# Weight conversions in other steps, operands split ahead by way of DRAM, sums spaced out: one change to a fused attention and two-MLP kernel

## The chip, the cores and the metric

The kernel runs on one core of a Trainium2 chip. The metric is device microseconds of one execution, the median of several. TensorE multiplies matrices (PE in the rows; PEld is its weight load, which runs beside it), VectorE (DVE), ScalarE (ACT) and GpSimd (POOL) work element by element, and DMA transfers are issued from the queues of SyncE (SPq) and ScalarE (ACTq).

## The reference

```python
# q, k, v: (8, 8, 576, 64);  w_in: (512, 2048);  w_out: (2048, 512), twice; the weights arrive as 64-bit floats
q_s = exp(q - max(q, -1));  q_s = q_s / (sum(q_s, -1) + 1e-9)
k_s = exp(k - max(k, 2));   k_s = k_s / (sum(k_s, 2) + 1e-9)
kv  = einsum('bhsd,bhse->bhde', k_s, v)
x   = einsum('bhsd,bhde->bhse', q_s, kv)       # then (4608 tokens, 512)
h = x @ w_in;   x = (h * clip(h + 3, 0, 6) / 6) @ w_out        # first MLP
h = x @ w2_in;  out = (h * sigmoid(h)) @ w2_out                # second MLP
```

## The kernel before

**Precision.** A float32 operand is split into an upper part, rounded to TensorE's reduced format by a copy on ScalarE, and a lower part, the rest, by a subtraction on VectorE. Each product is three matmuls (upper by upper, upper by lower, lower by upper), each 128x128 by 128x512.

**First MLP** (up to about 957 us). Tokens go in 9 blocks of 512. A block takes 16 steps, one for each 128 columns of `w_in`. A step holds `mm1` (L485, 12 matmuls of L492), `gate` (L542: Relu on ScalarE L505, product on VectorE L512, upper part on ScalarE L520, lower part on VectorE L523), and `mm2` of the step before (L551, 12 matmuls of L562). Steps are numbered 0 to 15 within a block here. Everything is emitted in program order, and each engine works in that order.

Attention runs inside these steps, one unit (a pair of heads for one block) for every four steps. A unit begins in step 1, 5, 9 or 13, and its part number r counts steps from there. At r = 0, after the gate, `k_max` (L285) makes VectorE find the maxima of k, which the transposition `k_turn` (L294, L296) on TensorE takes at r = 1, right after that step's `mm1`. At r = 3 (steps 0, 4, 8 and 12), `q_store` (L416) sends a transposed tile to DRAM from ScalarE's queue (zd<-qz, L417). At r = 4 (steps 1, 5, 9 and 13) ScalarE, at the top of its step, waits for that store, issues `q_load`'s four loads (qt<-zd, L423), scales a small tile (`kv_upper`, L353), and only then comes to the Relu of the step. From the third block on, r = 4 of a unit and r = 0 of the next one fall in the same step.

In the same steps the weights of the second MLP are prepared, two jobs a block (`Parts`, L172). A job converts two tiles from 64 bits (`convert`: two ScalarE passes L114 and L116, three VectorE passes L120, L127 and L131), makes four sums on GpSimd (`sums`, L196), and splits and stores four tiles (`upper` L202, `lower` L206 and L208, ws<-sp). `load_w` fetches the raw tiles (L97, wi_raw).

**Second MLP** (957 to 1721 us). Tokens go in four pairs of blocks, and each pair does its two matrix products by a scheme with 7 block products in place of 8 (`second_mlp`, L960). A pair has an inner stage (L991, w2_in) and an outer stage (L1089, w2_out) of 56 product steps each, six matmuls to a step. Work is put at planned times in units of such a step, with `when(t, fn)`, and emitted in the order of these times; t0 is the start of a pair, start[0] that of its outer stage. In the outer stage every step needs its own moving operand split first: `split` (ScalarE, L1070) and `split_low` (VectorE, L978, gsp<-g) stand `LOOK` = 3 steps ahead. GpSimd turns the stored tiles into the next products' operands (T2 and T4) inside `split_low`, and `join` combines finished products on VectorE, all of one product at once. The outer stage also prepares the 14 operand tiles of the next pair, `op[name]` (`x_steps`, L905): it loads them from `yd` (L893), sums on GpSimd (L903, 128x1024), and splits in place (L899 ScalarE, L900 VectorE, xo). Weights stream through six ring tiles of 512 KB, refilled when used (`fetch`, L875, ring<-ws). `spare` holds eight 128x512 tiles. A last block goes through the second MLP in the plain way, from about 1626 us.

## Time and profile before

| | us |
|---|---|
| median of 3 runs (1722.03 to 1725.01) | 1724.02 |
| the profiled execution | 1723.13 |
| its span in the profile | 1721.3 |
| PE busy | 1631.2 (95%) |
| DVE busy | 1080.8 (63%) |
| ACT busy | 741.7 (43%) |
| POOL busy | 357.4 (21%) |

The 1.8 us between span and execution lie around the program. TensorE is busy in all but 90 us, so a wait elsewhere matters where TensorE ends up waiting for it. Its granted clock is 0.986 of full speed over the span.

### The profile page before, as it was taken

Reading aid. Unit: us, or ns where it says so; the run is one execution under the profiler, and the core shown is the slowest. Engines: PE = TensorE matmul, PEld = TensorE weight load, DVE = VectorE, ACT = ScalarE, POOL = GpSimd, SP = SyncE. Lnnn points to the kernel's source line nnn. Section 1 sums busy time; section 2 is a strip of 40 time slices with the busy share of each in tenths; the row PEclk is TensorE's granted clock in tenths of the full one; section 3 lists DMA queues with packets and bytes.
Section 4 is the critical chain, followed back from the end, with each engine's and each line's share of the span. In section 5 each row is a group of like instructions: output and inputs, shape, how many; then the busy total and the mean of one; then the engine's idle time right before and its main releaser. Section 6 shows DMA issues by size and latency. Waiting matters only on the chain.

```text
span 1721.3 us, 21607 instructions
## 1 busy us (share of the span) xinstructions
PE 1631.2 (95%) x7612; PEld 1312.2 (76%) x7612; DVE 1080.8 (63%) x1748; ACT 741.7 (43%) x1285; POOL 357.4 (21%) x290
## 2 busy tenths in 40 slices
PE   6999999898998989989999999899999999999998
PEld 4777777677876777878788886788678867886887
DVE  8997556565564556555545568856885687568522
ACT  6885334343443434333334434434443444344322
POOL 2111101111011110111111127112701370135000
PEclk9999999999999999999999999999999999999999
DMA  9812434444443445323342656466546655669730
GB/s 274 299 41 65 138 107 125 113 132 126 139 121 96 134 110 162 118 76 103 98 159 74 220 191 213 163 205 215 212 163 208 204 208 176 210 204 348 259 122 25
DMA packets 273498, 273.53 MB, mean 159 GB/s; under 512 B 111216, under 2 KB 195184, under 8 KB 273392
## 3 DMA queue, kind: packets, MB, share of 16 engines
q1 hardware_dynamic: 210432, 256.92, 45.3%
q10 hardware_dynamic: 62960, 15.25, 3.9%
q8 instruction: 60, 0.98, 0.2%
q14 instruction: 46, 0.38, 0.1%
HBM read 212.60 MB, written 59.51 MB: 158 GB/s over the span
## 4 chain that ended last, share of the span: by engine, by line
PE 70%; DVE 17%; ACT 4%; DMA 4%; issue 2%; POOL 1%; ACTq 1%; SPq 0%; DVEq 0%; POOLq 0%
PE h L492 19%; PE y L562 17%; PE pb L991 17%; PE pb L1089 11%; DVE gsp L978 5%; PE y L564 2%; DMA zd<-qz 2%; DVE fa L127 2%; PE pa L450 1%; DVE fa L131 1%; DMA qt<-zd 1%; DVE r L512 1%; DVE xo L900 1%; ACTq L423 1%; DVE g L523 1%
## 5 line engine op out<-in xcount | busy, mean ns | idle before, releaser
L492 PE MATMUL h<-x,wi 128*128 128x512 f32 x1920 | 472.6, 393 | 2.3 <-DVE wi L152 1.0
L562 PE MATMUL y<-g,wo 128*128 128x512 f32 x1728 | 432.6, 400 | 2.4 <-ACT g L520 2.4
L492 PEld LDWEIGHTS h<-x,wi 128*128 128x128 f32 x1920 | 356.6, 188 | 79.3 <-DVE wi L152 2.8
L562 PEld LDWEIGHTS y<-g,wo 128*128 128x128 f32 x1728 | 329.6, 193 | 73.4 <-ACT g L520 2.8
L1089 PE MATMUL pb<-gsp,ring 128*128 128x512 f32 x1344 | 326.2, 399 | 24.8 <-DVE gsp L978 20.9
L1089 PEld LDWEIGHTS pb<-gsp,ring 128*128 128x128 f32 x1344 | 251.8, 190 | 97.9 <-DVE gsp L978 43.3
L991 PE MATMUL pb<-xo,ring 128*128 128x512 f32 x1344 | 313.3, 391 | 0.0
L991 PEld LDWEIGHTS pb<-xo,ring 128*128 128x128 f32 x1344 | 250.5, 188 | 51.7
L512 DVE SCALAR_TENSOR_TENSOR r<-r,h 128x512 f32<-128x512 f32 x128 | 87.9, 687 | 231.4 <-ACT r L505 230.8
L978 DVE TENSOR_TENSOR gsp<-g,gsp 128x512 fp32r<-128x512 f32 x192 | 178.8, 957 | 40.9 <-ACT gsp L1070 40.5
L1070 ACT CAST gsp<-g 128x512 fp32r<-128x512 f32 x192 | 117.0, 620 | 108.2 <-PE pb L1089 74.3
L505 ACT ACTIVATE r<-h 128x512 f32<-128x512 f32 x144 | 85.9, 597 | 169.7 <-PE h L492 164.6
L520 ACT CAST g<-r 128x512 fp32r<-128x512 f32 x144 | 89.4, 621 | 143.1 <-DVE r L512 131.0
L523 DVE TENSOR_TENSOR g<-r,g 128x512 fp32r<-128x512 f32 x144 | 103.1, 716 | 53.4 <-ACT g L520 43.8
L978 POOL TENSOR_TENSOR spare<-g,g 128x512 f32<-128x512 f32 x32 | 43.2, 1351 | 352.0 <-DVE g L978 315.2
L978 DVE TENSOR_TENSOR g<-r,pb 128x512 f32<-128x512 f32 x96 | 65.9, 686 | 70.8 <-ACT r L1004 70.4
L375 POOL TENSOR_TENSOR qe<-qraw,qm 128x512 f32<-128x512 f32 x34 | 36.0, 1058 | 352.4 <-DVE qm L367 281.7
L397 POOL TENSOR_TENSOR qe<-qe,qs 128x512 f32<-128x512 f32 x36 | 37.6, 1045 | 315.3 <-DVE qs L392 311.2
L1004 ACT ACTIVATE r<-pb 128x512 f32<-128x512 f32 x96 | 57.5, 599 | 91.1 <-DVE pb L978 74.8
L120 DVE TENSOR_SCALAR fa<-fa 128x512 uint32<-128x512 uint32 x64 | 28.0, 438 | 69.5 <-ACT fa L114 69.2
L353 ACT ACTIVATE kv<-pa,rs 64x64 fp32r<-64x64 f32 x56 | 17.3, 309 | 105.1 <-DMA qt<-zd 49.0
L978 DVE TENSOR_TENSOR U<-pb,s 128x512 f32<-128x512 f32 x64 | 44.2, 691 | 24.1 <-PE pb L991 22.3
(150 smaller groups left out, 1608.4 us busy)
## 6 DMA issues: line engine op xcount, KB each, us to landing
ring<-ws SPq DMA_DIRECT2D x224, 512.0 KB, 3.7
ws<-sp SPq DMA_DIRECT2D x128, 256.0 KB, 2.5
yd<-o SPq DMA_DIRECT2D x36, 256.0 KB, 2.9
wi_early<-in_moe_w_in_dram SPq DMA_DIRECT2D x16, 512.0 KB, 9.0
wo_early<-in_moe_w_out_dram SPq DMA_DIRECT2D x16, 512.0 KB, 9.4
wi_raw<-in_moe_w_in_dram SPq DMA_DIRECT2D x16, 512.0 KB, 4.4
wo_raw<-in_moe_w_out_dram SPq DMA_DIRECT2D x16, 512.0 KB, 4.1
out_dram<-o SPq DMA_DIRECT2D x32, 256.0 KB, 3.2
```

Of the source, the lines that this page charges most:

```text
L397: eng.tensor_tensor(out=e, in0=e, in1=s.to_broadcast([P, 2 * NCH, D]), op=ALU.mult)
L492: nc.tensor.matmul(h, w[:, a, c, :], x[:, e, c, :], start=(c == 0 and n == 0), stop=(c == NC - 1 and n == 2),)
L505: nc.scalar.activation(self.r, self.h, AF.Relu, bias=3.0)
L512: nc.vector.scalar_tensor_tensor(out=r, in0=r, scalar=6.0, in1=h, op0=ALU.min, op1=ALU.mult)
L520: nc.scalar.copy(self.g[:, 0], self.r)
L523: nc.vector.tensor_tensor(out=self.g[:, 1], in0=self.r, in1=f32(self.g[:, 0]), op=ALU.subtract)
L562: nc.tensor.matmul(y[c], w[:, a, cs], g[:, e, :], start=st, stop=sp)
L978: (eng or nc.vector).tensor_tensor(out=out, in0=a, in1=b, op=how)
L991: nc.tensor.matmul(to, ws_[:, a], e[:, c], start=p in ("P1", "P6", "P5") and c == 0 and m == 0, stop=c == 1 and m == 2, skip_group_check=True,
L1004: nc.scalar.activation(r, d[b, n, key], AF.Sigmoid)
L1070: nc.scalar.copy(t[:, 0], source(p, i))
L1089: nc.tensor.matmul(d[b, p][m], w[:, a, m * P : (m + 1) * P], t[:, e], start=i == 0 and k == 0, stop=i == NPR - 1 and k == 2, skip_group_ch ...
```

## The change

Three things are done, and the order of TensorE's instructions stays the same.

1. In the first MLP a job's conversions stand in steps 3 and 4, and 11 and 12, of each block's 16, where they stood in 1 and 2, and 8 and 9. The four sums follow in the second conversion's step, and the four splits and stores take that step and the three after it (before: 4 to 7 and 11 to 14). `load_w` moves along.
2. In the second MLP the next pair's operands are made in halves (`x_ahead`): four loads into `spare`, four GpSimd sums (128x512), seven splits into the rotating tiles of the outer splits, and 14 stores to a new DRAM buffer `xd`. For the second pair both halves are made in the first pair's inner stage. For later pairs the first half is made in the outer stage of two pairs before, the second in the inner stage of the pair before. 14 transfers (`x_fetch`) then bring the finished operands into `op` in the outer stage.
3. The T2 and T4 sums go to planned times of their own (`next_t2` every 1.8 steps, `next_t4` every 2.6), `c22` moves from VectorE to GpSimd, the joins are one step apart, splits stand 4 steps ahead over five tiles in place of four.

```diff
+    xd = dram.tile([2, 7, P, 2, 2, BLK], F32, name="xd")
...
-    LOOK = 3
+    LOOK = 4
...
-                add(d[b, n, "22"], d.pop((b, n, "U3")), d[b, n, "22"])
+                add(d[b, n, "22"], d.pop((b, n, "U3")), d[b, n, "22"], ALU.add, nc.gpsimd)
...
-            when(e["P7"] + 1.1, lambda: sig(b, n, "22"))
+            when(e["P7"] + 1.6, lambda: sig(b, n, "22"))
...
+        def split_tile():
+            n = turns[0] % 5
+            turns[0] += 1
+            if n == 4:
+                return [
+                    att.tile([P, BLK], F32R, tag=tag, bufs=1, name="gsp") for tag in ("ke", "qe")
+                ]
+            if n < 2:
                 t = gs.tile([P, 2, BLK], F32R, tag="g", name="gsp")
             else:
+                t = att.tile([P, 2, BLK], F32R, tag=("sp", "qT")[n - 2], bufs=1, name="gsp")
+            return [t[:, 0], t[:, 1]]
...
         def split_low(b, p, i):
             t = d["sp", b, p, i]
-            add(t[:, 1], source(p, i), f32(t[:, 0]), ALU.subtract)
-            if p == "P1":
-                g1 = g_of(2 * i)
-                add(g1[:, 0], op["spare"][:, i], g1[:, 0], ALU.add, nc.gpsimd)
-            if p == "P6":
...
+            add(t[1], source(p, i), f32(t[0]), ALU.subtract)
+
+        def next_t2(i):
+            g1 = g_of(2 * i)
+            add(g1[:, 0], op["spare"][:, i], g1[:, 0], ALU.add, nc.gpsimd)
...
+        def x_ahead(j, c, side, t, step):
+
+            st = {n: op["spare"][:, 3 + m] for m, n in enumerate(("B12", "B22", "B11", "B21", "T"))}
+
+            def load(n):
+                jj, h = j + (n[2] == "2"), int(n[1] == "2")
+                nc.sync.dma_start(st[n], yd[jj, 2 * h + c])
+
+            def high(n, src):
+                d["x", n] = split_tile()
+                nc.scalar.copy(d["x", n][0], st[src])
+
+            def low(n, src):
+                hi, lo = d.pop(("x", n))
+                add(lo, st[src], f32(hi), ALU.subtract)
+                to = xd[side, XS.index(n)]
+                nc.sync.dma_start(to[:, 0, c], f32(hi))
+                nc.sync.dma_start(to[:, 1, c], f32(lo))
...
+                when(t + m * step + 0.3, lambda n=n, src=src: high(n, src))
+                when(t + m * step + 0.9, lambda n=n, src=src: low(n, src))
+
+        def x_fetch(side, n, low):
+            nc.sync.dma_start(f32(op[n][low]), xd[side, XS.index(n)][:, low])
...
+                if p == "P1":
+                    when(start[0] + 1.4 + 1.8 * i, lambda i=i: next_t2(i))
+                if p == "P6":
+                    when(start[0] + 18.4 + 2.6 * i, lambda i=i: next_t4(i))
...
+                if b == 0:
+                    x_ahead(j + 2, 0, side, t0 + 1.0, 1.8)
+                    x_ahead(j + 2, 1, side, t0 + 15.0, 1.8)
+                else:
+                    x_ahead(j + 2, 1, side, t0 + 4.0, 3.2)
+                if b + 2 < BB:
+                    x_ahead(j + 4, 0, 1 - side, start[0] + 22.0, 4.0)
+                for m, n in enumerate(XS):
+                    for low in range(2):
+                        when(
+                            start[0] + 3.1 + 6.0 * m + 3.0 * low,
+                            lambda n=n, low=low, side=side: x_fetch(side, n, low),
+                        )
...
-            for r in range(7):
-                parts_at[(n // 2 + 1) * NF + 1 + 7 * (n % 2) + r] = (n, r)
+            for r in range(5):
+                parts_at[(n // 2 + 1) * NF + 3 + 8 * (n % 2) + r] = (n, r)
...
-            if r is not None and r >= 3:
-                made[job].upper(r - 3)
-                made[job].lower(r - 3)
+            if r:
+                made[job].upper(r - 1)
+                made[job].lower(r - 1)
```

Line numbers of the changed kernel are one higher up to about line 1060. On ScalarE, in steps 8 and 9 of a block before the change, k's exponential (L326) is followed by a conversion, the gate, the store, the loads and a second conversion ahead of the next Relu (L505):

```order
L326 ACTIVATE ke<-ke 128x640
L114 ACTIVATE fa<-wi_raw 128x512
L116 ACTIVATE fr<-wi_raw 128x512
L505 ACTIVATE r<-h 128x512
L520 CAST g<-r 128x512
L417 DMA zd<-qz 128x512
L423 DMA qt<-zd 32x16x32 x4
L353 ACTIVATE kv_93<-pa,rs 64x64 x2
L114 ACTIVATE fa<-wi_raw 128x512
L116 ACTIVATE fr<-wi_raw 128x512
L505 ACTIVATE r<-h 128x512
```

The same two steps after the change have neither conversion:

```order
L327 ACTIVATE ke<-ke 128x640
L506 ACTIVATE r<-h 128x512
L521 CAST g<-r 128x512
L418 DMA zd<-qz 128x512
L424 DMA qt<-zd 32x16x32 x4
L354 ACTIVATE kv_93<-pa,rs 64x64 x2
L506 ACTIVATE r<-h 128x512
```

After the change the conversions stand in the two steps that end with another unit's store (here steps 3 and 4, likewise 11 and 12), and the first split (L203) follows the store:

```order
L461 CAST x<-pa 128x512
L115 ACTIVATE fa<-wi_raw 128x512
L117 ACTIVATE fr<-wi_raw 128x512
L506 ACTIVATE r<-h 128x512
L521 CAST g<-r 128x512
L327 ACTIVATE ke<-ke 128x640
L115 ACTIVATE fa<-wi_raw 128x512
L117 ACTIVATE fr<-wi_raw 128x512
L506 ACTIVATE r<-h 128x512
L521 CAST g<-r 128x512
L418 DMA zd<-qz 128x512
L203 CAST sp<-fa 128x512
```

So no conversion stands any more behind a store's wait; one stands ahead of the store in steps 4 and 12. On VectorE, in the outer stage of the first pair before the change, the 1024-wide splits of the next pair's operands (L900) stand between the outer splits (gsp):

```order
L978 TENSOR_TENSOR gsp<-g_8615,gsp 128x512
L900 TENSOR_TENSOR xo<-spare,xo 128x1024
L978 TENSOR_TENSOR gsp<-g_8691,gsp 128x512
L978 TENSOR_TENSOR gsp<-g_8770,gsp 128x512
L978 TENSOR_TENSOR gsp<-g_8238,gsp 128x512
L978 TENSOR_TENSOR gsp<-g_8313,gsp 128x512
L900 TENSOR_TENSOR xo<-spare,xo 128x1024
```

After the change 18 outer splits follow each other here, and from then on half-size splits for a later pair (gsp<-spare, 128x512) and joins (vbuf, fin, kbuf) come in between:

```order
L979 TENSOR_TENSOR gsp<-g_8356,gsp 128x512
L979 TENSOR_TENSOR gsp<-spare,gsp 128x512
L979 TENSOR_TENSOR gsp<-g_8450,gsp 128x512
L979 TENSOR_TENSOR gsp<-g_8548,gsp 128x512
L979 TENSOR_TENSOR vbuf_95<-pb,kbuf_94 128x512
L979 TENSOR_TENSOR gsp<-g_8629,gsp 128x512
L979 TENSOR_TENSOR fin<-pb,fin 128x512
```

The 1024-wide operations have left this stage; the half-size ones stand in its second part, in the first two pairs.

## Rows read from the trace of the kernel before

**Rows 1.** Waits of PE, whole run: us in total, times, longest.
```profile
PE pa L296 <- DVE m L291: 37.1, 11, 5.9
PE pb L1089 <- DVE gsp L978: 20.9, 16, 2.3
PE y L562 <- ACT g L520: 2.4, 1, 2.4
```

**Rows 2.** PE's timeline: start, us, instruction, count, idle before it.
```profile
172.09 2.88 PE L492 MATMUL h<-x,wi 128*128 128x512 f32 x12
186.80 0.27 PE L296 MATMUL pa<-ident,m 128*128 128x128 f32 x1
196.13 2.88 PE L492 MATMUL h<-x,wi 128*128 128x512 f32 x12
216.50 0.44 PE L296 MATMUL pa<-ident,m 128*128 128x128 f32 x1 [5.50 <-DVE m L291]
```

**Rows 3.** Windows behind the first and the last long wait: busy times, PEclk, DMA.
```profile
216.50:222.00 5.50, 5.50 (x20) 4.57 (x21) 3.03 (x7) 1.17 (x3) 1.05 (x1) 0.70 0.02 4
741.00:747.00 6.00, 6.00 (x20) 4.88 (x20) 2.88 (x7) 1.24 (x3) 1.04 (x1) 0.63 0.00 0
```

**Rows 4.** The chain that ended last, 201 to 217 us: start, us, what.
```profile
201.49 4.60 DMA zd<-qz
...
206.74 2.11 DMA qt<-zd
...
209.54 0.66 ACT fa L114
210.20 0.58 ACT fr L116
...
211.53 0.69 DVE fa L131
...
216.06 0.30 DVE m L291
```

**Rows 5.** ACT's timeline, a step's store and loads without a conversion.
```profile
176.42 0.34 ACTq L417 DMA_DIRECT2D zd<-qz  x1
...
178.47 2.92 ACTq L423 DMA_DIRECT2D qt<-zd  x4
```

**Rows 6.** DVE's timeline, the end of `k_max` in that step.
```profile
186.15 0.29 DVE L291 TENSOR_TENSOR m<-m,kbuf 128x128 f32<-128x128 f32 x1
```

**Rows 7.** SP's timeline ahead of the store at 201.49.
```profile
200.91 0.37 SPq L97 DMA_DIRECT2D wi_raw<-in_moe_w_in_dram  x1
```

**Rows 8.** Windows of the first, second and fourth pair: PE, PEld, DVE, ACT, POOL busy, PEclk, DMA.
```profile
962.44:1125.18 162.74, 153.86 (x662) 122.81 (x661) 120.51 (x150) 70.83 (x115) 58.14 (x36) 1.00 0.57 197
1125.18:1294.59 169.41, 162.91 (x706) 129.87 (x705) 120.72 (x150) 73.24 (x121) 58.17 (x36) 0.98 0.58 199
...
1463.98:1625.91 161.93, 159.21 (x706) 128.41 (x705) 109.07 (x147) 69.29 (x118) 46.28 (x32) 1.00 0.76 259
```

**Rows 9.** The chain that ended last, inner stages.
```profile
962.44 70.73 PE pb L991 x312
...
1137.92 0.44 PE pb L1125 x4
```

**Rows 10.** DVE's timeline, outer stage of the first pair.
```profile
1069.42 7.94 DVE L978 TENSOR_TENSOR gsp<-g,gsp 128x512 fp32r<-128x512 f32 x4
```

**Rows 11.** Windows there, and in the fourth pair's outer stage; columns as in rows 8.
```profile
1068.00:1077.00 9.00, 5.10 (x19) 3.33 (x19) 8.72 (x5) 4.51 (x8) 9.00 (x6) 1.00 0.25 72
...
1560.00:1590.00 30.00, 27.56 (x118) 21.58 (x118) 24.51 (x30) 14.08 (x24) 12.10 (x8) 1.00 0.99 353
```

**Rows 12.** Tile gsp, VectorE: ns of one, min/median/max.
```profile
L978 DVE TENSOR_TENSOR gsp<-g,gsp x192: 675/692/2895, 1031.6 to 1621.2; 128x512 fp32r<-128x512 f32 x192
```

**Rows 13.** A GpSimd sum in the page's costliest groups: busy us, mean ns of one, idle before.
```profile
L978 POOL TENSOR_TENSOR spare<-g,g 128x512 f32<-128x512 f32 x32 | 43.2, 1351 | 352.0 <-DVE g L978 315.2
```

**Rows 14.** DMA issues of the page: KB each, median us from issue to landing.
```profile
ring<-ws SPq DMA_DIRECT2D x224, 512.0 KB, 3.7
```

More of the change, by code (lines that the diff above doesn't have):

```diff
@@ new lines, in next_t2, with next_t4, total @@
+        def next_t2(i):
+            g1 = g_of(2 * i)
+            add(g1[:, 0], op["spare"][:, i], g1[:, 0], ALU.add, nc.gpsimd)
+        def next_t4(i):
+            g1 = g_of(2 * i)
+            add(g1[:, 0], g1[:, 0], g_of(2 * i + 1)[:, 0], ALU.subtract, nc.gpsimd)
+        XS = ("B11", "T2", "T1", "B21", "T3", "B22", "T4")
+        def x_ahead(j, c, side, t, step):
[12 more added lines that the diff above has]
+                nc.sync.dma_start(to[:, 1, c], f32(lo))
+            def total(to, x, y, how):
+                add(st[to], st[x], st[y], how, nc.gpsimd)
+            for m, n in enumerate(("B22", "B12", "B11", "B21")):
+                when(t - 4.0 + 0.3 * m, lambda n=n: load(n))
+            when(t + 0.02, lambda: total("T", "B22", "B12", ALU.subtract))
+            when(t + 0.03, lambda: total("B12", "B12", "B11", ALU.subtract))
+            when(t + 3 * step + 0.02, lambda: total("T", "T", "B11", ALU.add))
+            when(t + 5 * step + 0.02, lambda: total("T", "B21", "T", ALU.subtract))
+            for m, (n, src) in enumerate((
+                ("B22", "B22"), ("B11", "B11"), ("T3", "T"), ("T1", "B12"), ("T2", "T"),
+                ("B21", "B21"), ("T4", "T"),
+            )):
+                when(t + m * step + 0.3, lambda n=n, src=src: high(n, src))
+                when(t + m * step + 0.9, lambda n=n, src=src: low(n, src))
@@ L1093, in outer, with joins, tile, do @@
                     )
-        def join(b, p):
-            for m in range(2):
+        def joins(b, p, t):
+            def tile(m, n):
+                return fixed[4 * m + n]
+            def do(m, name):
                 one, two, three, c22 = fixed[4 * m : 4 * m + 4]
-                if p == "P1":
-                    nc.scalar.copy(one, d[b, p][m])
-                if p == "P6":
-                    add(two, d[b, p][m], one)
-                    add(three, d[b, "P7"][m], two)
-                if p == "P5":
-                    add(c22, d[b, p][m], three)
-                    add(two, d[b, p][m], two)
-                if p == "P3":
-                    add(two, d[b, p][m], two)
-                if p == "P4":
-                    add(three, three, d[b, p][m], ALU.subtract)
-                if p == "P2":
-                    add(one, d[b, p][m], one)
-            if p != "P7":
-                d.pop((b, p))
-            if p == "P6":
-                d.pop((b, "P7"))
+                at = d[b, p][m]
+                if name == "one":
+                    nc.scalar.copy(one, at)
+                elif name == "U2":
+                    add(two, at, one)
+                elif name == "U3":
+                    add(three, d[b, "P7"][m], two)
+                elif name == "C22":
+                    add(c22, at, three)
+                elif name in ("U4", "C12"):
+                    add(two, at, two)
+                elif name == "C21":
+                    add(three, three, at, ALU.subtract)
+                else:
+                    add(one, at, one)
+            names = {
+                "P1": ("one",), "P7": (), "P6": ("U2", "U3"), "P5": ("C22", "U4"),
+                "P3": ("C12",), "P4": ("C21",), "P2": ("C11",),
+            }[p]
+            for k, (name, m) in enumerate((name, m) for name in names for m in range(2)):
+                when(t + k, lambda m=m, name=name: do(m, name))
         def turn(j, k, bank=bank):
@@ L1166, in second_mlp @@
                 if i == NPR - 1:
-                    when(t + 1.3, lambda b=b, p=p: join(b, p))
+                    joins(b, p, t + 1.3)
             j = 1 + 2 * b
             if b + 1 < BB:
-                do = x_steps(j + 2)
-                base = start[0]
-                for x, name in (
[3 rows of a table removed]
-                ):
-                    when(base + x, do[name])
+                side = b % 2
+                if b == 0:
+                    x_ahead(j + 2, 0, side, t0 + 1.0, 1.8)
+                    x_ahead(j + 2, 1, side, t0 + 15.0, 1.8)
+                else:
+                    x_ahead(j + 2, 1, side, t0 + 4.0, 3.2)
[7 more added lines that the diff above has]
+                        )
                 for k in range(2 * NCH):
```

24 lines of the change are left out of this document (10 added, 14 removed), and 3 rows, old and new, of the table base.

## The prediction

> **What bounds the kernel now.** I read the page's table of engines first: TensorE is busy in all but 90 us, and the change leaves its instructions and their order alone. So the time can only change where TensorE waits or runs slowly, and the next views were the waits of TensorE and the windows with its clock.
>
> In the first MLP one wait carries nearly everything: `k_turn` waits for the end of `k_max`, 11 times, 37.1 us, and one `mm2` adds 2.4 [rows 1]. Six of the 11 last about 5.5 us, once a block, five about 0.8. Behind each long one the granted clock falls to its lower level for some microseconds: 0.70 over 5.5 us behind the first, 0.63 over 6 us behind the last [rows 3]. While TensorE is busy all the time, a window of length L at mean clock c loses (1 - c)L: 1.7 and 2.2 us for these two, 13.4 for all six. **The first MLP thus holds 37.1 + 2.4 + 13.4 = 52.9 us.**
>
> The chain shows what is late [rows 4]. The store at 201.49 takes 4.60 us to land, the four loads are issued until 208.85, then ScalarE converts (0.66 + 0.58) ahead of the Relu, VectorE works through the conversion ahead of the gate's product, and `k_max`, last in that queue, ends at 216.36. TensorE was there at 211.00 [rows 2]. Step 5 shows the same without a conversion: store at 176.42, 4.33 us after its step's first matmul; landing seen 2.05 us later; loads issued until 181.39 [rows 5]; `k_max` done at 186.44 [rows 6]; TensorE there at 186.80 [rows 2]. That is 0.36 us to spare, 14.71 us after the start of the store's step.
>
> In the second MLP I compare a pair with its matmuls. 312 of them took 70.73 us, 0.2267 each, and a transposition group 0.44 [rows 9]. 672 matmuls and eight groups make 155.9. The second pair takes 169.4, so 13.5 too much; the third is like it; the fourth has 6.0; the first has 660 matmuls and no groups in its window, 149.6, so 13.1 [rows 8]. **Together 46.1 us.** 20.9 of it are waits for `split_low` [rows 1], the clock's 0.98 takes 3.4 in each of two pairs [rows 8], the rest is spread over shorter delays. The cause is in the outer stage: four splits took 7.94 us, 1.99 each [rows 10], where the median is 0.692 [rows 12], in a stretch in which GpSimd was busy without a gap [rows 11]. There VectorE cannot give TensorE one split in each product step of six matmuls, 1.36 us.
>
> **The conversions.** Removed from steps 1, 2, 8 and 9: both late sequences above lose their conversion behind the store. What remains in steps 1 and 9 is step 5's sequence, and without the split that step 5 has ahead of `k_max` (about 0.7). It waits only when the store lands over 1 us later than 2.05. I take nothing for these steps. Their old length, 52.9, is the gain.
>
> What is added stands in steps 4 and 12. There a conversion now comes ahead of the gate whose end starts the store, as it does today in step 8, where the store came 201.49 - 196.13 = 5.36 us after the first matmul [rows 2, 4], so 1.03 later than 4.33. Of these, 0.36 are spare: **0.67 us of new wait**, in each place with a `k_turn` behind it. Units 9, 11, ... 29 make 11 such places: 7.4 us. The low bound is nothing (the split ahead of k's subtraction is gone from the step before, which lets the conversion start earlier). The high bound is a store that lands as today's late one, 4.60 in place of 2.05: 3.2 us in each place, 35 in all. I stay near the low end, for the reason under the first rival. Waits this short would leave the clock where it is, as the short waits of today do. The sums move to the end of steps 4 and 12, where they slow the gate's VectorE operations, not `k_max`; that is inside the bounds. **Net: 52.9 - 7.4 = 45.5 us gained.**
>
> **The operands.** Gone from each outer stage of three pairs are seven 1024-wide splits on VectorE and ScalarE and four 1024-wide sums on GpSimd. In the stretch of rows 10 this was what kept GpSimd busy without a gap. Their work returns as twice as many operations of half the width, most of it in the inner stages, where TensorE waits for nothing; there VectorE was busy 120.5 us of the first pair's 162.7 over both stages [rows 8], and `c22` leaves it. In the outer stages of the first two pairs seven half-size splits remain, from step 22.
>
> I count that stretch, steps 22 to 37, 20.4 us long: 15 outer splits, 4 half-size ones and 8 joins on VectorE, 27 operations of 0.69, 18.6 us; beside them 6 T4 sums and 3 others, 12.2 us at 1.351 [rows 13]. With GpSimd busy throughout, a split costs 1.3 more than its median [rows 10, 12]. Let the stretch take T: T = 18.6 + 19 x 1.3 x 12.2/T gives 29 us, 8.6 too long. Splits run 3.8 steps ahead, 5.2 us, less about 1.6 for the two operations of one: 3.6 to spare. So up to 5 us of wait in each of these pairs, down to none if the overlap costs half as much; I take 3. In the last two pairs (no half-size splits) the same formula gives 22.8 us, within the lead. At the start of every outer stage the T2 sums (8 x 1.351 in 19 us) still slow the splits, though the lead is a step longer; I leave 3 us a pair.
>
> The Trainium skill's page "SBUF — State Buffer", section "SBUF: two separate sides", says that VectorE with two SBUF inputs and a reading GpSimd exclude each other for whole instructions. That agrees with 1.99, which is 0.69 plus about one sum. By the rule the stretch would take 25 us (splits and sums in turn) to 31 (joins too), a wait of 1 to 7 us where I take 3.
>
> **The transfers.** Per pair 8 loads and 28 stores of 256 KB and 14 fetches of 512 KB are added, and 4 loads of 512 KB go. The ring alone moves 512 KB in two steps, 193 GB/s. In the first pair's inner stage, steps 0 to 27, loads and stores add 9.4 MB in 36.7 us: 450 GB/s. The trace sustains 353 [rows 11]. The surplus is 3.6 MB, a delay of 10 us at the end. A ring tile is refilled five tiles, 13.6 us, before use and lands in 3.7 [rows 14], so 9.9 are spare. I take 2 us, bounds 0 and 6. In the outer stages of the first two pairs the sum is 417 GB/s over 34 us, a delay of 6 us, hidden. SyncE's queue is in order: a store waits for its split, and ring refills wait behind it; that uses the same 9.9 us.
>
> Left over: 4 x 3 + 2 x 3 + 2 = 20 us. **Net: 46.1 - 20 = 26.1 us gained.** The joins, spread out, are in the count above.
>
> **Sum.** 1723.13 - 45.5 - 26.1 = 1651.5 for an execution like the profiled one. The median lies 0.9 higher: 1652.
>
> **Rivals.**
>
> *The store lands late in the new place* (steps 4 and 12). Today's late store followed a raw-weight load by 0.6 us [rows 4, 7]. After the change such a load is still issued near this store. For it: it is the same pair of transfers. Against it: on SyncE's queue the load follows that of k, which waits for a subtraction of the step before, so it should start some 2 us or more ahead of the store. Price: 11 x 3.2 = 35 in place of 7.4, so 1680. The Trainium skill's page "DMA: Bandwidth & Descriptors", section "Queues, rings and completion order", says that a DMA engine's signal of completion lands after all its earlier writes, of other queues too; the 4.60 agrees.
>
> *The outer stages keep their excess*: GpSimd and VectorE still collide (T2, T4 and half-size splits), the clock falls again. With 40 of 46.1 left: 1672. With both rivals at once 1700.
>
> *Slower: the transfers become the bound of the first three pairs.* They would move 143 MB there (ring 88, fetches 22, stores 22, the rest 10), in some 501 us today. To lose the 45.5 of the first MLP and 3.4 more, these pairs must take 550 us, so the engines must deliver under 260 GB/s. Against it: 353 over 30 us [rows 11]. For it: a queue in order, in which one late store holds all refills. From 260 down it decides; at 250 the time is about 1745.
>
> **How the numbers follow.** 64% for the forecast, whose own range is 1638 to 1666; 14% for the late store, 14% for the kept excess, 4% for both, 4% for slower. A difference of 0.2%, 3.4 us, is about what a measurement here can tell. Only the last case, and a share of the one before that goes worse than counted, end at or above 1720: faster 0.93, same 0.02, slower 0.05. The range reaches down to no new waits and half the left-over (1637, say 1636) and up past the two middle rivals: 1690.
>
> **What would show it.** Right: the six 5.5 us waits and the lower clock behind them are gone, 11 small waits of `k_turn` at most, no GpSimd operation of 1024, pair windows of about 158, 162, 159 and 159 us. Wrong: waits of `k_turn` of 2 us and more, TensorE waiting for the ring or for `split_low` from step 22 on, the clock below 1 in an outer stage.

## The result, and the profile after

The changed kernel takes 1661.47 us (median of 4 runs), the kernel before 1723.13 beside it: a ratio of 0.964, 95% interval 0.9623 to 0.9656. The forecast was 1652 us. The profiled execution's span fell from 1721.3 to 1660.3 us.

The waits of TensorE in the changed kernel, which answer to [rows 1]:

```profile
engine line waited for: us in total, times, longest us
PE ph L297 <- DVE m L292: 8.5, 3, 7.4
PE pa L297 <- DVE m L292: 7.4, 18, 1.0
PE pb L992 <- DVE U L979: 6.8, 1, 6.8
PE pb L1142 <- DVE gsp L979: 3.4, 6, 1.0
...
PE pb L1142 <- ACT gsp L1081: 1.7, 3, 0.7
```

The six waits of 5.5 us for `k_max` are gone (pa, 7.4 us in all, none over 1.0), and so is most of the waiting for `split_low` (3.4 for 20.9). New is one wait of 6.8 us for U, in the first inner stage. The windows of the first MLP and of the four pairs, with the columns of [rows 8]:

```profile
170.00:906.00 736.00, 728.59 (x3615) 592.99 (x3614) 443.31 (x810) 307.22 (x540) 123.41 (x120) 1.00 0.42 125
917.79:1084.26 166.47, 156.25 (x661) 124.99 (x660) 120.22 (x156) 73.42 (x129) 79.52 (x52) 0.97 0.89 318
1084.26:1246.78 162.52, 159.77 (x705) 128.40 (x705) 115.84 (x149) 72.25 (x128) 72.17 (x48) 1.00 0.85 298
1246.78:1405.06 158.28, 158.06 (x706) 128.79 (x705) 112.85 (x142) 69.34 (x121) 65.37 (x44) 1.00 0.80 276
1405.06:1564.96 159.90, 158.65 (x705) 128.59 (x705) 107.86 (x139) 68.00 (x118) 59.12 (x40) 1.00 0.77 262
```

The forecast was pairs of 158, 162, 159 and 159 us. The second to fourth have 162.5, 158.3 and 159.9; the first has 166.5. For what follows I cut the time at starts of matmuls: the last `mm1` of the first MLP, the first outer product of each pair, and the first inner product of the next. In the changed kernel the first two cuts are these rows of TensorE's timeline:

```profile
906.68 2.88 PE L493 MATMUL h<-x,wi 128*128 128x512 f32 x12
...
1001.80 1.52 PE L1142 MATMUL pb<-gsp,ring 128*128 128x512 f32 x6
```

So its first inner stage is 95.12 us long. All stages, in us:

```
                    before   after   difference   forecast
start to last mm1   951.40  906.68     -44.72      -45.5
first inner stage    82.96   95.12     +12.16       +2
outer stage, pair 1  90.66   82.30      -8.36
outer stage, pair 2  90.65   83.75      -6.90
outer stage, pair 3  90.65   79.52     -11.13
outer stage, pair 4  83.17   81.16      -2.01
four outer stages   355.13  326.73     -28.40      -28.1
other inner stages  236.25  236.27       0.0         0
rest                 95.56   95.50      -0.1         0
```

The forecast sum was 10.6 us too large, and 10.2 of that lie in the first inner stage. There the queues of SyncE (SPq), ScalarE and VectorE read:

```profile
914.50 1.94 SPq L878 DMA_DIRECT2D ring<-ws  x4
916.48 2.36 SPq L1103 DMA_DIRECT2D spare<-yd  x4
...
926.01 1.82 SPq L575 DMA_DIRECT2D yd<-o  x4
```

```profile
924.04 0.62 ACT L1107 CAST gsp<-spare 128x512 fp32r<-128x512 f32 x1 [9.78 <-DMA spare<-yd]
924.57 1.08 ACT L572 ACTIVATE o<-y 128x512 f32<-128x512 f32 x2
...
926.04 0.60 ACT L1023 COPY s<-pb 128x512 f32<-128x512 f32 x1
929.59 1.28 ACT L1005 ACT_TABLE_LOAD   x1 [2.95 <-DMA yd<-o]
```

```profile
926.50 0.68 DVE L979 TENSOR_TENSOR U<-pb,s 128x512 f32<-128x512 f32 x1
```

Read them together. The four ring fetches (2 MB) and, behind them, four early loads go out at 914.5 to 918.8. ScalarE reaches the first early split (L1107) and stands there for 9.78 us until its load has landed. Behind it stand the copies that empty TensorE's banks (L572, L1023); U needs the second of them, and TensorE needs U. The stores of y go out only at 926.01, since their source was copied at 924.57, and the first sigmoid waits for them: its output takes one of the rotating tiles in which y's copies lie (both are allocated under the tag `t2k`), so a store must have landed first. The clock fell too, in the wait and behind it, to near its lower level (2.4 GHz is 1.00, 1.2 is 0.50):

```profile
922.00:927.20 5.20, 0.00 (x0) 0.00 (x0) 2.51 (x5) 2.60 (x5) 2.33 (x2) 0.61 0.88 329
927.20:935.00 7.80, 7.76 (x21) 6.12 (x22) 3.70 (x5) 2.80 (x4) 2.71 (x3) 0.60 1.02 355
```

Of the stage's 12.16 us, 8.4 are idle time of TensorE (this wait and two short ones), and about 3.1 (0.40 of 7.8) are the low clock behind the long wait.

### The profile page after: what moved, and what is told of

Same layout as the page of the kernel before. It is cut to its first block, busy times and chain, and to the rows that moved or that the text cites. A ratio compares the mean times of both kernels' runs of the same rounds, so it can differ in the third digit from the quotient of the medians.

```text
span 1660.3 us, 22032 instructions
## 1 busy us (share of the span) xinstructions
PE 1613.2 (97%) x7612; PEld 1302.0 (78%) x7612; DVE 1075.3 (65%) x1737; ACT 740.2 (45%) x1306; POOL 422.4 (25%) x334
## 4 chain that ended last, share of the span: by engine, by line
PE 64%; DVE 17%; ACT 6%; DMA 6%; issue 4%; ACTq 3%; POOL 0%; SPq 0%; DVEq 0%; POOLq 0%
PE pb L992 17%; PE h L493 17%; PE y L563 14%; PE pb L1142 10%; DVE gsp L979 6%; ACTq L424 3%; PE y L565 2%; DMA zd<-qz 2%; DMA xd<-gsp 2%; DVE r L513 2%; PE pa L451 1%; ACT g L521 1%; ACT r L506 1%; DVE fa L128 1%; DVE fa L132 1%
## 5 line engine op out<-in xcount | busy, mean ns | idle before, releaser
L563 PE MATMUL y<-g,wo 128*128 128x512 f32 x1728 | 420.6, 392 | 0.0
L563 PEld LDWEIGHTS y<-g,wo 128*128 128x128 f32 x1728 | 321.3, 188 | 67.0
L992 PE MATMUL pb<-xo,ring 128*128 128x512 f32 x1344 | 317.1, 394 | 8.4 <-DVE U L979 6.8
L1142 PE MATMUL pb<-gsp,ring 128*128 128x512 f32 x1344 | 316.5, 393 | 6.1 <-DVE gsp L979 3.4
L979 DVE TENSOR_TENSOR gsp<-g,gsp 128x512 fp32r<-128x512 f32 x192 | 169.3, 906 | 45.2 <-ACT gsp L1081 44.1
L506 ACT ACTIVATE r<-h 128x512 f32<-128x512 f32 x144 | 86.2, 599 | 152.5 <-PE h L493 133.7
L979 DVE TENSOR_TENSOR gsp<-spare,gsp 128x512 fp32r<-128x512 f32 x74 | 83.9, 1163 | 18.0 <-ACT gsp L1107 18.0
L979 POOL TENSOR_TENSOR s<-U,s 128x512 f32<-128x512 f32 x32 | 43.5, 1359 | 154.5 <-DVE U L979 83.3
L197 POOL TENSOR_TENSOR ws_sum<-fa 128x256 f32<-128x256 f32 x32 | 29.4, 920 | 163.7 <-ACT r L506 96.2
```

The source lines that it names most:

```text
L506: nc.scalar.activation(self.r, self.h, AF.Relu, bias=3.0)
L563: nc.tensor.matmul(y[c], w[:, a, cs], g[:, e, :], start=st, stop=sp)
L979: (eng or nc.vector).tensor_tensor(out=out, in0=a, in1=b, op=how)
L992: nc.tensor.matmul(to, ws_[:, a], e[:, c], start=p in ("P1", "P6", "P5") and c == 0 and m == 0, stop=c == 1 and m == 2, skip_group_check=True,
L1142: nc.tensor.matmul(d[b, p][m], w[:, a, m * P : (m + 1) * P], t[e], start=i == 0 and k == 0, stop=i == NPR - 1 and k == 2, skip_group_check ...
```

## The experiments

Two theories stand against each other for the first inner stage. *Queue*: an operation that waits for a late load stands at the head of an in-order queue. *Transfers*: the DMA engines are the bound, and the order only decides who waits. The table holds what was measured, all against the kernel before in the same session; "mm1" is the start of the last `mm1`, then come the first inner and the four outer stages.

```
                              us   ratio  interval          mm1  inner  outer 1 to 4
changed kernel           1661.47  0.9640  .9623 to .9656  906.7  95.1  82.3 83.8 79.5 81.2
e1_first_split_later     1657.47  0.9616  .9599 to .9634  906.3  91.4  82.2 82.5 79.5 81.2
e2_conversions_alone     1680.50  0.9747  .9731 to .9764  905.0  85.3  91.6 90.6 90.6 83.1
e3_operands_alone        1701.99  0.9871  .9856 to .9886  951.6  89.6  83.1 83.1 79.5 81.2
e4_operands_as_before    1668.27  0.9674  .9660 to .9689  904.5  86.2  87.3 87.4 87.4 81.2
e5_loads_in_first_mlp    1657.94  0.9614  .9601 to .9627  906.0  92.9  83.1 84.1 79.5 81.2
e6_no_late_loads         1654.70  0.9591  .9577 to .9604  905.2  89.4  82.8 82.4 79.5 81.2
e7_sums_as_before        1662.02  0.9636  .9623 to .9649  904.8  95.3  84.4 83.0 80.3 80.8
e8_load_behind_store     1669.51  0.9680  .9667 to .9694  914.9  94.0  83.3 82.2 79.5 81.2
e9_spread                1655.47  0.9599  .9586 to .9612  909.9  86.1  83.3 83.1 79.5 81.2
e10_transfers_alone      1672.96  0.9700  .9687 to .9714  905.1  90.4  87.4 87.2 87.7 81.2
e11_operations_alone     1670.28  0.9684  .9671 to .9697  904.0  88.0  87.3 87.3 87.2 81.2
e12_lookahead_3          1663.11  0.9646  .9632 to .9659  905.3  94.5  84.6 83.9 80.0 80.8
```

The kernels whose first MLP is that of the changed one have mm1 between 904.0 and 906.7, so 2.7 us there mean nothing. The first inner stage of the changed kernel and of the three that leave its early halves alone (e7, e8, e12) takes 94.0 to 95.3, so about 1.3 us there mean little.

**The parts one by one.** The kernel before with the new numbers of steps (and the moves that go with them):

```diff
-            for r in range(7):
-                parts_at[(n // 2 + 1) * NF + 1 + 7 * (n % 2) + r] = (n, r)
+            for r in range(5):
+                parts_at[(n // 2 + 1) * NF + 3 + 8 * (n % 2) + r] = (n, r)
```

> The kernel before, with the conversions moved to their new steps and nothing else. Theory (the two parts are independent, the first MLP's gain is the conversions' alone): the six waits of 5.5 us and the low clock behind them go, the first MLP ends 44.7 us earlier, the four pairs stay at 663 us, the whole is 1678.5 (1676 to 1681). Rival (a part of the first MLP's gain comes from the other edits, or the second MLP starts worse when the first ends in another state, since the last weight stores now come in the last step): 1682 or more.

1680.5 us: as the theory has it. The first MLP's gain is the conversions' alone. But its first inner stage is 2.3 us longer than before, and the reason lies in this edit. The same place in the kernel before and in this run, SyncE's and ScalarE's rows:

```profile
954.31 1.90 SPq L877 DMA_DIRECT2D ring<-ws  x4
962.52 1.80 SPq L574 DMA_DIRECT2D yd<-o  x4
...
964.59 1.28 ACT L1004 ACT_TABLE_LOAD   x1 [0.17 <-DMA yd<-o]
```

```profile
906.58 5.82 SPq L208 DMA_DIRECT2D ws<-sp  x4
912.80 1.94 SPq L877 DMA_DIRECT2D ring<-ws  x4
916.09 2.17 SPq L574 DMA_DIRECT2D yd<-o  x4
...
922.93 1.28 ACT L1004 ACT_TABLE_LOAD   x1 [4.93 <-DMA yd<-o]
```

The last weight job now ends in the last step, its stores (ws<-sp) hold the ring's 2 MB until 912.80, and the stores of y, 1.3 us behind them instead of 6.3, land late: ScalarE's first sigmoid waits 4.93 us for them, not 0.17, and TensorE then waits 2.0 us for U.

The other way round, the changed kernel with that diff undone:

> The changed kernel with the conversions back in their old steps: the x operands, the sums and the lookahead as changed. Theory: the first MLP is as long as before; the pairs gain their 16 us, and up to 9 more, since the last weight job then ends two steps before the first MLP does and the fetches that fill the ring are not held by its stores, so the early split of the first pair waits less: 1699 to 1706. Rival (the early split is late whatever stands ahead of it): the first pair keeps its 166 us, 1706 to 1708.

1702.0: inside the theory's bounds. With the ring's fetches no longer late the first inner stage still takes 89.6, 6.7 more than before, so the early halves (their transfers and operations) cost there on their own.

Then the changed kernel with the operands made as before in the outer stage:

```diff
-                if b == 0:
-                    x_ahead(j + 2, 0, side, t0 + 1.0, 1.8)
...
+                do = x_steps(j + 2)
+                base = start[0]
...
```

> The changed kernel with the next pair's operands made as before, in the outer stage with 1024-wide sums and splits; conversions, spacing of sums and joins, the longer lookahead and the fifth tile stay. Theory A (the wide sums and splits made the excess of the outer stages, and the way by DRAM removed it): the pairs return to 655 to 663 us, the whole to 1669 to 1678, with waits for the low half of the outer splits. Theory B (the spacing and the lookahead removed it, the way by DRAM only added transfers): the first pair shrinks to 155 us, the others stay at 158 to 163, the whole is 1648 to 1655.

1668.3, a little under A's bounds: both were right in part. Of the 28.4 us that the outer stages lost, 11.8 stay (355.13 to 343.30), 16.6 come from the way by DRAM. That way costs 8.9 in the first inner stage (86.18 to 95.12); so it is worth some 7 us where it could be 16.6. In the outer stage without it VectorE is busy in 79.4 of 88 us, and the listed waits of TensorE there, 3.7 us, are all for its splits:

```profile
990.00:1078.00 88.00, 83.92 (x346) 64.53 (x345) 79.40 (x82) 40.91 (x65) 42.44 (x23) 0.98 0.58 197
```

**The first inner stage.** The changed kernel with the early halves later:

```diff
-                    x_ahead(j + 2, 0, side, t0 + 1.0, 1.8)
-                    x_ahead(j + 2, 1, side, t0 + 15.0, 1.8)
+                    x_ahead(j + 2, 0, side, t0 + 6.0, 1.8)
+                    x_ahead(j + 2, 1, side, t0 + 20.0, 1.8)
```

> The changed kernel, with the first pair's early splits (and the loads ahead of them) five product steps later: the first half from step 6, the second from step 20, so that the loads come after the four ring fetches that fill the ring. Theory (an early split at the head of ScalarE's in-order queue waits for a load that lands late, and the copies that drain TensorE's banks stand behind it): the 6.8 us wait of the inner product on U and the half clock around it go, the first pair's window falls from 166.5 to about 157 us, the whole to 1652 (1649 to 1655). Rival (the transfers of the inner stage, some 450 GB/s asked for, are the bound, and the order only decides who waits): the waits move to the ring or to other copies, the first pair stays at 163 us or more, the whole at 1658 to 1664.

The stage takes 91.4: 3.7 better, not 9. The wait for U falls to 2.0 us, what it is in the two kernels without early splits (2.0 and 2.6), but others of up to 1.5 us come in. Neither theory explains this alone. Next, the loads of the first early half issued in the first MLP's last block (steps 10 to 13):

```diff
+        early_x = {10: (1, "B22"), 11: (0, "B12"), 12: (2, "B11"), 13: (3, "B21")}
...
+            nc.sync.dma_start(
+                op["spare"][:, 3 + m], yd[3 + (n[2] == "2"), 2 * int(n[1] == "2")]
+            )
```

> The changed kernel, with the four loads of the first pair's first early half issued in steps 10 to 13 of the last block of the first MLP, where their tiles are free; the splits, their stores and everything else stay in place, and the bytes are the same. In the changed kernel the first inner stage, from the last mm1 to the first outer product, took 95.1 us; with the splits later 91.4; with the operands as before 86.2. Theory (ScalarE's queue is held by a split whose load is late): the wait of 6.8 us on U falls to the 2 us or so that the run without early splits has there too, the stage takes 87 to 90 us, the whole 1653 to 1657. Rival (the engines' transfers bound the stage): the same bytes, so the stage stays at 91 us or more, the whole at 1657 to 1662, with waits further on.

92.9: the theory falls in this form. No split waits for a load now, yet the wait for U is still 4.8 us, since the sigmoid waits for the stores of y, behind 2 MB of ring and the first early stores:

```profile
914.23 2.16 SPq L878 DMA_DIRECT2D ring<-ws  x4
916.49 0.41 SPq L1119 DMA_DIRECT2D xd<-gsp  x1
...
917.69 2.28 SPq L575 DMA_DIRECT2D yd<-o  x4
...
926.68 1.28 ACT L1011 ACT_TABLE_LOAD   x1 [7.69 <-DMA yd<-o]
```

So I put two of the ring's fetches behind the stores of y as well (in addition, both halves start later, the second's loads earlier):

```diff
-        for k in range(2, 6):
+        for k in range(2, 4):
             fetch(k)
...
-        when(1.95, lambda: (mm2(last), finish(0, NB - 1)))
+        when(1.95, lambda: (mm2(last), finish(0, NB - 1), fetch(4), fetch(5)))
```

> As the run with loads in the first MLP, and in addition the fifth and sixth ring fetch come behind the stores of the last block's y instead of ahead of them, and the second early half starts at step 19.5 with loads 6.5 steps ahead (in the changed kernel step 15, 4 ahead). Theory (every loss of the first inner stage is an in-order queue behind a late transfer): no wait over 1 us in that stage, which takes 83 to 86 us as in the kernel before (83.0), the whole 1649 to 1653. Rival (the transfers bound it, at 350 to 400 GB/s over some 60 us): the stage stays at 89 us or more, the whole at 1655 or more.

1654.7, the fastest of all, and faster than the changed kernel beyond both intervals; but 89.4 us is at the rival's bound. Two runs on top of the one with operands as before (86.2) then took the parts of the cost apart, first the transfers alone:

```diff
+                if b == 0:
+                    x_moves(j + 2, 0, t0 + 1.0, 1.8)
+                    x_moves(j + 2, 1, t0 + 15.0, 1.8)
...
+            def low(n, src):
+                to = xd[0, XS.index(n)]
+                nc.sync.dma_start(to[:, 0, c], st[src])
+                nc.sync.dma_start(to[:, 1, c], st[src])
```

> The run with the operands as before (first inner stage 86.2 us; 95.1 in the changed kernel), with the 8 loads and 28 stores of the first pair's early halves put back at their planned steps, but no split and no sum: what is stored is the raw x, and nobody reads it. Theory (transfers are what costs, as bound or as late arrival): the stage takes 89 to 93 us with waits for the ring or for copies behind the store of y, the whole 1671 to 1676. Rival (only the operations in ScalarE's and VectorE's queues cost): 86 to 87.5 us, the whole 1667 to 1670.

90.4: the transfers alone cost 4.2 us, mostly in one place. TensorE waits 5.65 us for U, where it waited 2.6 in the run with the operands as before, and its granted clock is 0.80 over the next 8.1 us, where that run has 1.00. ScalarE stands 8.56 us for the stores of y. These stood in SyncE's queue: y was copied by 916.8, but ahead of its stores is the first early store (xd<-spare), which waits for its load.

```profile
922.33 0.32 SPq L1142 DMA_DIRECT2D xd<-spare  x1
...
923.23 1.90 SPq L575 DMA_DIRECT2D yd<-o  x4
```

```profile
926.64 1.28 ACT L1005 ACT_TABLE_LOAD   x1 [8.56 <-DMA yd<-o]
```

So this run too has an operation that waits for a late load at the head of a queue, and its 4.2 us are not the price of the bytes alone. Then the operations alone:

```diff
+            src = op["spare"][:, 3]
+
+            def high(m):
+                d["x", m] = split_tile()
+                nc.scalar.copy(d["x", m][0], src)
...
+            def total(to):
+                add(op["spare"][:, to], src, src, ALU.subtract, nc.gpsimd)
```

> The run with the operands as before, with the 14 half-size splits and 8 sums of the first pair's early halves put back at their planned steps, but no load and no store: the splits read a tile that is there, and nobody reads what they make. Theory (without a late load the operations find room, VectorE was busy in some 60% of this stage): 86 to 88 us, the whole 1667 to 1671. Rival (the operations themselves delay the copies that drain TensorE's banks): 90 us or more, the whole 1672 or more.

88.0: the operations alone cost 1.8, as the theory has it and little more than this stage scatters. The two make 6.0; both at once cost 8.9. The 2.9 between come only with both together; the split that waits for its load at the head of ScalarE's queue exists only there and is the likely cause, but no run shows it by itself. Last, the transfers spread over 40 steps, and a raw weight load moved (next part):

```diff
-                    x_ahead(j + 2, 0, side, t0 + 2.2, 1.8, False)
-                    x_ahead(j + 2, 1, side, t0 + 19.5, 1.8, True, 6.5)
+                    x_ahead(j + 2, 0, side, t0 + 2.2, 2.4, False)
+                    x_ahead(j + 2, 1, side, t0 + 23.0, 2.8, True, 6.5, ("B22", "B12", "B11", "B21", "T"))
...
+            before, at_end = parts_at.get(n - 2, (None, None))
```

> As the run with no late loads (first inner stage 89.4 us; its transfers were busy 0.97 to 1.06 from 916 to 966 us), with the two early halves of the first pair spread over 40 product steps in place of 31, the second half's tiles in another order so that its slots are free in time; by the count of the prediction the stage then asks for some 358 GB/s in place of 450. And the second raw weight load of each job comes two steps later, behind the loads of z, where no store of z is under way. Theory (a saturated stretch of transfers delays loads and ring refills, and the in-order queues pass the delay on): the stage takes 86 to 87.5 us, as with the operands made as before (86.2); the waits of k_turn sum to 3 to 5 us in place of 7, the whole is 1648 to 1652. Rival (the added splits and sums on ScalarE, VectorE and GpSimd delay the copies that drain the banks, whatever the transfers do): the stage stays at 88.5 us or more, the whole at 1652 or more.

The stage takes 86.1, the theory's figure, the same as without early splits, with all of them in it. The whole is past the rival's bound, but by the other edit: the first MLP became 4.7 us longer. The same 50 us, 916 to 966, in four kernels (windows, columns as above): the changed one, the operands as before, the transfers alone, the spread.

```profile
916.00:966.00 50.00, 41.63 (x169) 33.17 (x168) 30.30 (x44) 20.50 (x37) 26.63 (x18) 0.90 0.98 356
```

```profile
916.00:966.00 50.00, 47.37 (x208) 38.57 (x207) 26.00 (x40) 17.61 (x31) 17.63 (x14) 1.00 0.67 228
```

```profile
916.00:966.00 50.00, 44.35 (x190) 36.28 (x189) 23.64 (x37) 16.62 (x29) 15.49 (x12) 0.93 0.98 360
```

```profile
916.00:966.00 50.00, 48.19 (x208) 38.47 (x207) 34.05 (x48) 24.02 (x44) 24.15 (x17) 1.00 0.98 351
```

The DMA engines are as full in the last as in the first (0.98; 351 and 356 GB/s), and TensorE is idle for 1.8 us in the one and 8.4 in the other. A full set of DMA engines is no loss by itself here; it is one through what stands in order behind a late transfer.

**The store of z.** In the changed kernel it lands late in steps 0 and 8, where a raw weight load is issued shortly ahead of it. I put that load behind the store in the program:

```diff
-            if r == 4 and job + 1 < 2 * NPR:
-                load_w(1, 2 * made[job + 1].i + 1, made[job + 1].o)
...
+            before, at_end = parts_at.get(n - 1, (None, None))
+            if at_end == 4 and before + 1 < 2 * NPR:
+                load_w(1, 2 * made[before + 1].i + 1, made[before + 1].o)
```

> The changed kernel with the second raw weight load of each job issued behind the store of z in the next step, not ahead of it at the end of the step before. Theory (that load and k's, both ahead of the store, make it land 3.1 to 4.4 us after its issue in steps 0 and 8, and k_turn then waits 0.2 to 1.0 us): the landing there falls to 2 to 3 us, the sum of k_turn's waits from 7.4 us (8.5, 7.0 and 6.4 in the other runs with these conversions) to 3 to 5, the first MLP ends 2 to 4 us earlier. Rival (k's load alone makes it late): the sum stays at 6 to 9 us, the end where it is.

Neither: 8 us slower, and `k_turn` waits 15.8 us in all. The queues of SyncE and ScalarE tell why; first the changed kernel, then this one, from k's and the raw weight load to the store (zd<-qz) and the loads that wait for its landing (qt<-zd):

```profile
199.39 0.62 SPq L98 DMA_DIRECT2D wi_raw<-in_moe_w_in_dram  x1
200.11 0.52 SPq L238 DMA_DIRECT2D kbuf<-in_k_dram  x1
...
201.75 0.33 ACTq L418 DMA_DIRECT2D zd<-qz  x1
205.07 1.97 ACTq L424 DMA_DIRECT2D qt<-zd  x3
```

```profile
198.61 0.58 SPq L238 DMA_DIRECT2D kbuf<-in_k_dram  x1
...
199.94 0.59 SPq L98 DMA_DIRECT2D wi_raw<-in_moe_w_in_dram  x1
...
200.93 0.33 ACTq L418 DMA_DIRECT2D zd<-qz  x1
205.34 1.97 ACTq L424 DMA_DIRECT2D qt<-zd  x3
```

The load is on SyncE's queue, the store on ScalarE's. Nothing holds SyncE there, so the load still went out ahead of the store, now behind k's loads and 0.99 us ahead instead of 2.36, and the store was seen landed 4.41 us after its issue in place of 3.32. The bytes ahead of the store are the same; that the raw load goes last is what changed. So it has a part in the lateness. The spread run separates the two loads further. Its raw load was meant to come two steps later. In step 8 nothing holds SyncE, and it still went out behind k's, 1.0 us ahead of the store, which landed after 4.6 to 5.2 us: `k_turn` waits 7.1 us behind these five stores, of 10.2 in all. In step 0 SyncE is held by the stores of y, so only k's loads go out ahead of the store of z:

```profile
248.23 0.65 SPq L242 DMA_DIRECT2D kbuf<-in_k_dram  x1
...
249.93 0.33 ACTq L418 DMA_DIRECT2D zd<-qz  x1
251.97 1.29 ACTq L424 DMA_DIRECT2D qt<-zd  x2
```

There the store is seen landed after 2.04 us, in all five blocks that load k, and `k_turn` does not wait behind it. So k's loads alone do not make it late, and e8's rival falls. In the changed kernel's later blocks, where no k is loaded any more, a raw load 2.2 to 2.4 us ahead alone gives 2.4 to 2.6 us. For step 0 the spread run thus has a better place than the changed kernel; for step 8 none was found.

**Sums and lookahead.** The sums at each split, as before; and the splits three steps ahead, as before (`LOOK = 3`):

```diff
+            if p == "P1":
+                next_t2(i)
+            if p == "P6":
+                next_t4(i)
```

```diff
-    LOOK = 4
+    LOOK = 3
```

> The changed kernel with GpSimd's sums of the outer stage (T2 and T4) issued right behind each split as before, not spaced out. Outer stages of the changed kernel: 82.3, 83.8, 79.5, 81.2 us, before 90.7, 90.7, 90.7, 83.2, with the operands as before but the rest changed 87.3, 87.4, 87.4, 81.2. Theory (the wide operations of the operands and the short lookahead made the excess; the spacing adds little once they are gone): the outer stages grow by 0 to 1 us each, the whole is 1661 to 1665. Rival (the spacing brought the 3.3 us a stage that the run with operands as before still gained): 3 us or more in each of the first three, the whole 1669 to 1674.

> The changed kernel with the outer splits three product steps ahead, as before, in place of four; the fifth tile, the spacing of sums and joins and the operands as changed. Outer stages of the changed kernel: 82.3, 83.8, 79.5, 81.2 us. Theory (the longer lead is what took 3.3 us from each outer stage in the run with the operands as before): the first three grow by 1 to 3 us each, the whole is 1664 to 1670. Rival (the joins, one a step in place of all at once, took them): 0 to 0.5 us each, the whole 1660 to 1663.

The outer stages grow by 1.8 us in all in the first (2.1, -0.8, 0.8, -0.3), by 2.5 in the second (2.3, 0.2, 0.5, -0.4). Of the first the theory is right in the sum, though the first stage alone is over its 1 us; of the second the first stage follows the theory, the next two the rival. The times, 1662.0 and 1663.1, can't be told from the changed kernel's. What of the 11.8 us in the run with operands as before is whose (fifth tile, joins one a step, lookahead, spacing) stays open.

## Why the prediction was right, and where it was not

*The conversions* (45.5 forecast, 44.7 measured): right with its mechanism. The long waits and the low clock behind them are gone. The 7.4 us of new waits are 7.4, but by two errors that cancel. TensorE's timeline shows 18 waits of `k_turn`; two of them:

```profile
188.10 0.30 PE L297 MATMUL pa<-ident,m 128*128 128x128 f32 x1 [0.97 <-DVE m L292]
...
310.86 0.30 PE L297 MATMUL pa<-ident,m 128*128 128x128 f32 x1 [1.04 <-DVE m L292]
```

The 11 places behind the stores of steps 4 and 12 are there (the first row is one), with 3.35 us in all, 0.30 each where I had 0.67. The other 7 stand behind the stores of steps 0 and 8 (the second row), 4.0 us, where I had taken nothing. That the sum is right is luck.

*The first rival* (the store lands late) came true in another place: in steps 0 and 8 it lands 3.1 to 4.4 us after its issue (3.32 in the row at 201.75 above) where I had allowed 3.05, and most of that is hidden. The rule of the Trainium skill's page "DMA: Bandwidth & Descriptors", section "Queues, rings and completion order", that was set beside this rival (a signal of completion lands behind the engine's earlier writes) is in line with 4.41 us with the raw load last ahead of the store against 3.32 with k's last; it doesn't say how much.

*The operands in the outer stages*: right in the sum, in part by errors that cancel. With 342 matmuls at 0.2267 [rows 9] an outer stage is 77.5 us; the four are 16.6 over that, where 18 were forecast (6, 6, 3, 3) and 4.8, 6.2, 2.0 and 3.6 measured.

The 3 us for the T2 sums are 1.9, in every pair. The list of waits does not show them: it holds idle times over 0.15 us, and here a step loses 0.3 us with less idle time than that. In steps 9 to 14 the sums on GpSimd follow each other without a gap, 1.70 us each, the splits beside them come at the same pace, and a product step, 1.36 us long, has to wait for one. VectorE's splits, GpSimd's sums, and a window of the first pair (columns of [rows 8]):

```profile
1012.60 11.45 DVE L979 TENSOR_TENSOR gsp<-spare,gsp 128x512 fp32r<-128x512 f32 x8
```

```profile
1010.40 11.91 POOL L979 TENSOR_TENSOR g<-spare,g 128x512 f32<-128x512 f32 x7
```

```profile
1014.04:1024.16 10.12, 9.91 (x37) 6.29 (x36) 10.12 (x9) 4.69 (x8) 8.27 (x5) 1.00 0.96 354
```

The window runs from the start of one matmul to that of the 36th behind it: 36 matmuls, 8.16 us at 0.2267, take 10.12. The mechanism of this term was right, its size 1.9: 7.6 us in all in place of 12. In the third pair it is all there is.

What is left over is 9.0 us in place of 6. The listed waits for splits among them are 1.6 and 2.6 us in the first two pairs. Of each, 0.9 falls into the stretch that I counted (steps 22 to 37), behind VectorE with GpSimd's T4 sums beside it. That is inside my bounds (0 to 5) and at the edge of those by the Trainium skill's rule on SBUF (1 to 7), so it doesn't decide between the two; in the rows above a split and a sum in strict turn would take 1.98 us (0.69 and the 1.29 of an undisturbed sum), and 1.70 were measured. The other waits come from step 41 on, from something left out of the count: a split takes a tile over whose stores to DRAM have to land first. The tile view of `gsp` says for how long an engine, mostly ScalarE, stood idle for that in the whole run (us, times):

```profile
  DMA xd<-gsp: 27.1, 14
```

The rival of a kept excess is out, and so is that of transfers as the bound of all three pairs: they run at 276 to 318 GB/s, with two of the pairs at their forecast length.

*The transfers of the first pair*: here the prediction failed, at 2 us in place of 12.2. Its rate held in that stage (353 GB/s; 351 to 364 over the 50 us from 916 on in all runs that are full), though 353 is not the most that the engines give; in the first pair's outer stage the changed kernel moves more:

```profile
1052.00:1082.00 30.00, 29.25 (x127) 23.36 (x126) 21.08 (x33) 13.31 (x24) 3.24 (x3) 1.00 1.04 398
```

Wrong was the sentence that the surplus makes "a delay of 10 us at the end", against which the ring's spare 9.9 us stand. The delay comes at the start, where the ring's first 2 MB go out, and it falls on transfers that have nothing to spare: the stores of y, for which the first sigmoid waits, and the loads of the first early split, at the head of ScalarE's queue. The low clock behind the long wait was not in the forecast either. Of the 12.2, the conversions' move brought 2.3 (the ring is fetched late), the transfers 4.2, the operations 1.8, both together 2.9 more; the remaining 0.9 is the difference of the two runs without early splits (85.3 and 86.2), within what this stage scatters. The shares depend on the order in which they are counted: without the conversions' move the early halves cost 6.7, and the move then adds 5.5. I had asked what each queue holds for SyncE's, with the ring behind it, but not for ScalarE's, with the banks behind it.

## What to carry to other kernels

When a change adds an operation that waits for a load, list what stands behind that operation on its engine, not only what the load delays on the DMA side; a copy that empties one of TensorE's output banks (PSUM) behind it stops TensorE. At a seam between stages, look which transfers have no lead, and put the bulk fetches that have some behind them. An instruction's place in the program does not by itself fix its time against another queue: a load moved "behind" a store went out closer ahead of it, and came behind it only where its own queue was held. And add up small waits too: 1.9 us in each outer stage were on no list.

## What the runs showed of the hardware

DMA engines that are busy 0.98 of 50 us delivered 351 to 360 GB/s with 1.8 to 8.4 us of TensorE idle, so the share by itself does not say whether a kernel is bound by transfers. The Trainium skill's page "DMA: Bandwidth & Descriptors", section "Specifications", gives some 358 GB/s as the limit of HBM for a core. The runs stay near it over 50 us (351 to 364), but 398 over 30 us in the changed kernel is past it, so it is not the limit here. A store of 256 KB was seen landed after 2.05 us in a step without a raw weight load [rows 5], after 2.04 with k's loads 1.7 us ahead and no raw load, after 3.3 with a raw load of 512 KB issued 2.4 us ahead and k's loads between, after 4.4 with k's loads first and the raw load 1.0 us ahead. After 6.8 us without matmuls the granted clock was 0.60 over the next 7.8 us (0.61 over the last 5.2 of the wait itself), while in the run with spread transfers, with waits up to 0.9 us in the same stage, it stayed at 1.00. VectorE's splits (0.69 us alone) beside GpSimd's sums without a gap came at 1.70 us, no faster than the sums.
